# A statically ordered attention and channel-mix kernel: first steps in a new order, measured durations for its scheduler, and two more pairs loaded in blocks

## Chip, cores, metric

The kernel runs on one core of a Trainium2 chip. The metric is the device time of one execution in microseconds (us). Engines are written as in the profile: PE is TensorE (matmul), PEld its weight load, DVE VectorE, ACT ScalarE, POOL GpSimd, SPq the queue of SyncE, which issues most transfers. A position such as "at 40 us" is a time from the start of the profiled execution.

## The reference

Attention over 4 batches and 8 heads, 768 positions, head size 64, in which a query sees only keys of its own cluster; then an RWKV channel mix.

```python
q_assign = argmax(normalised q . normalised centroids)      # 16 clusters per head
k_assign = argmax(normalised k . normalised centroids)
scores = where(q_assign == k_assign, q @ k.T / 8, -1e9)
x = (softmax(scores) @ v), heads put side by side           # 4 x 768 x 512
xk = mu_k * x + (1 - mu_k) * x_prev                         # x_prev: one position earlier
xr = mu_r * x + (1 - mu_r) * x_prev
out = sigmoid(xr @ w_r) * (relu(xk @ w_k) ** 2 @ w_v)
```

## The kernel before

The 32 heads are worked off as 16 pairs (pair 0 to 15, four to a batch). Each pair runs a chain over five engines. The cluster equality is made part of the score matmul: the one-hot cluster rows of q and k are laid under the 64 rows of q and k, so that the contraction has 80 rows. To get the one-hot rows there, they make a "hop": SyncE writes them to DRAM (`hop<-oht`) and reads them back in another layout (`aug<-hop`).

```python
# rows layout (pairs 0 to 5): 2 loads of 384 KB, TensorE transposes, copies from PSUM
eng.dma_start(t[:, i, :]..., src[b, 2*j:2*j+2].rearrange("h (m p r) d -> p (h m) (r d)", p=128, r=2))
nc.tensor.matmul(ps[...], nat[n][:, g // 2, m:m + 128], ident, is_transpose=True, ...)   # trans_pe
# block layout (pairs 6 to 15): 8 loads of 96 KB in 128-byte pieces, VectorE transposes 32x32 blocks
nc.sync.dma_start(nat[n][32*a:32*a+32, i, :]..., x[a // 2, a % 2])                        # load_qk
nc.vector.transpose(qkT[n][:, g, :], nat[n][:, g // 2, ...])                              # trans
# then, for every pair
nc.gpsimd.tensor_scalar(augs[n % NR][0:64, g, par, :], in0=qkT[n][...], ...)              # casts, 8 of them
nc.tensor.matmul(ps[32*g:32*g+32, :], cblk[...], qkT[n][:, g, :], ...)                    # aff_mm
...  # aff_t, aff_max, aff_back on VectorE
nc.sync.dma_start(hop, aff[n])                                                            # hop_out
nc.sync.dma_start(augs[n % NR][64:64 + C]..., hop...)                                     # hop_in
nc.gpsimd.tensor_copy(vts[n % NR][...], vnat[n][...])                                     # vcast
...  # scores (PE), exps (ACT), values (PE), norm (DVE), xtr/xcopy, diff, lerp: xk and xr
```

The order in which each engine takes these pieces of work is made by a small list scheduler in the kernel's Python, when the kernel is built. Every piece of work has an engine, an assumed duration, dependencies and priorities; the scheduler simulates the engines and emits each piece at the earliest time it finds. On the chip each engine then runs its list strictly in that order and waits on semaphores where data is late.

```python
def plan(rings, held, free, moving, at):
    bus = dict(at=at)
    ...
        if k.key in moving:                       # a transfer
            bus["at"] = max(bus["at"], free[e] + 0.4) + moving[k.key]
            k.end = bus["at"] + 1.5
        else:
            k.end = free[e] + k.lat
...
task(("exp", t), "ACT", 0.525, lambda t=t: exps(t), deps=[("scores", t)], ...)
task(("vcast", n), "POOL", 1.2, lambda n=n: vcast(n), deps=[("vload", n)] + ..., ...)
```

The softmax here doesn't subtract the row's maximum and nothing guards it: scores larger than these inputs give would overflow.

Of the kernel before, what the change touches and what calls it, by code (L numbers as in the profile page):

```python
# [16 lines left out]
def kernel(  # L17
# [13 lines left out]
    nc = tc.nc  # L31
# [182 lines left out]
    def first_trans(t):  # L214
        if t == 0:
            qkT[0] = qktp.tile([128, 4, GW], F32, name="qkT")
        for i in range(2):
            g = 2 * i + t
            ps = ps_w.tile([128, GW], F32, name="trps0", tag="w") if t == 0 else \
                (ps_o.tile([128, GW], F32, name="trps1", tag="out2") if i == 0 else  # L220
                 ps_st.tile([128, GW], F32, name="trps2", tag="st"))
            for c2 in range(NCH // 2):
                m = t * GW + c2 * 128
                nc.tensor.matmul(ps[:, c2 * 128:(c2 + 1) * 128], nat[0][:, i, m:m + 128], ident,
                                 is_transpose=True, start=(c2 == 0), stop=(c2 == NCH // 2 - 1))
            if i == 0:
                nc.vector.tensor_copy(qkT[0][:, g, :], ps)
            else:
                nc.scalar.copy(qkT[0][:, g, :], ps)
            casts(0, g)  # L230

    def first_aff(t, i):
        if i == 0:
            first[t] = ps_w.tile([128, 2, NCH, C], F32, name="aff0", tag="w")
        ps = first[t]
        for c2 in range(NCH // 2):
            nc.tensor.matmul(ps[:, i, 2 * c2:2 * c2 + 2, :], qkT[0][:, 2 * i + t, c2 * 128:(c2 + 1) * 128],
                             cblk[:, t, :, :], start=True, stop=True)
# [221 lines left out]
    WK, WR, WV = 11.5, 36.0, 42.0  # L460
    TAIL = {"PE": 0.25 + MARGIN, "ACT": 0.2 + MARGIN, "DVE": 0.15 + MARGIN, "POOL": 0.15, "SP": 0.0}

    def plan(rings, held, free, moving, at):

# [12 lines left out]
        bus = dict(at=at)  # L477
# [36 lines left out]
        while done < len(order):  # L514
# [19 lines left out]
            if k.key in moving:  # L534
                bus["at"] = max(bus["at"], free[e] + 0.4) + moving[k.key]
                k.end = bus["at"] + 1.5
# [20 lines left out]
    with tc.manual_schedule():  # L557
# [11 lines left out]
        load_rows(2, nc.sync, nc.sync)  # L569
        make_identity(nc, ident)  # L570
        init_ring(0)
        nc.gpsimd.tensor_copy(identb, ident)
        def use_pe(m):
# [4 lines left out]
        use_pe(8)  # L578
# [15 lines left out]
        nc.tensor.transpose(cnt_ps.rearrange("d h c -> d (h c)"), cn_sb, ident)  # L594
        nc.vector.tensor_copy(cblk[0:64, :, 0, :], cnt_ps)
        nc.vector.tensor_copy(cblk[64:128, :, 1, :], cnt_ps)
        first_trans(0)
        use_pe(4)
        first_aff(0, 0)
        first_aff(0, 1)  # L600
        first_max(0)
        first_trans(1)
        use_pe(1)
# [3 lines left out]
        for i in range(1, NR):  # L607
            init_ring(i)
        for mu in (mu_k_sb, mu_r_sb):
            nc.vector.tensor_scalar(mu, in0=mu, scalar1=-1.0, scalar2=None, op0=ALU.add)  # L610
# [21 lines left out]
        def soon(n, near, far):  # L632
            return lambda at: near if n < NP or START[n] + 14 <= at else far

        T0 = 10.5
        task(("aff1", 0), "PE", 1.45, lambda: (first_aff(1, 0), first_aff(1, 1)), rank=0, new=[("w", "aff1")],
             uses=[("qkT", 0)], sub=-8)
        task(("aff1max",), "DVE", 0.7, lambda: first_max(1), deps=[("aff1", 0)], uses=["aff1"], rank=0, sub=-8)
        for i in range(2):
            task(("oh1", i), "PE", 0.4, lambda i=i: first_onehot(1, i), deps=[("aff1max",)], rank=0, sub=-8,  # L640
# [3 lines left out]
        task(("vcast", 0), "POOL", 1.2, lambda: vcast(0), rank=0, sub=10, uses=[("vnat", 0)])  # L644

        for n in range(1, NPAIR):
            rows = n < 6
# [3 lines left out]
            if n > 2:  # L651
# [4 lines left out]
                else:  # L656
                    for a in range(8):
                        task(("load", n, a), "SP", 0.6, lambda n=n, a=a: load_qk(n, a // 4, a % 4), rank=2, step=START[n] + 3 * a // 2,
                             sub=due[n], new=[("nat", ("nat", n))] if a == 0 else [], uses=[("nat", n)] if a else [],
                             behind=[("load", n, a - 1)] if a else [("load", n - 1) if n == 6 else ("load", n - 1, 7)])  # L660
                        moving["load", n, a] = 0.65
            task(("vload", n), "SP", 0.5, lambda n=n: load_v(n, nc.sync), rank=2, sub=due[n] + 4, step=due[n] - 16,
                 new=[("vnat", ("vnat", n))], behind=[("vload", n - 1)] if n > 1 else [])
            moving["vload", n] = 1.3
            task(("vcast", n), "POOL", 1.2, lambda n=n: vcast(n), deps=[("vload", n)] +
                 [("norm", k[1] // NCH) for k in old], uses=[("vnat", n)], rank=1, sub=due[n] + 2)
            qt = ("qkT", n)
            if rows:
                at = {1: 10.0, 2: 14.0}.get(n, 0.0)
                for t3 in range(3):  # L670
# [5 lines left out]
                    task(("tcp", n, t3), ce, 0.66 if ce == "DVE" else 0.52,  # L676
# [4 lines left out]
            else:  # L681
                for g in range(4):
                    task(("trn", n, g), "DVE", 0.55, lambda n=n, g=g: trans(n, g),
# [4 lines left out]
            for g in range(4):  # L688
                task(("cast", n, g), "POOL", 1.12, lambda n=n, g=g: casts(n, g), deps=[got[g]] + old, uses=[qt],
# [3 lines left out]
            task(("afft", n), "DVE", 0.6, lambda n=n: aff_t(n), deps=[("aff", n)], uses=[("affps", n)],  # L693
                 new=[("t1", ("t1", n))], rank=0, sub=sub)
            task(("affm", n), "DVE", 1.15, lambda n=n: aff_max(n), deps=[("afft", n)], uses=[("t1", n)],
                 new=[("ohn", ("ohn", n))], rank=soon(n, near, 3 if far else 0), sub=sub)
            task(("affb", n), "DVE", 0.58, lambda n=n: aff_back(n), deps=[("affm", n)], uses=[("ohn", n)],
# [13 lines left out]
        for t in range(NSTEP):  # L711
# [3 lines left out]
            task(("scores", t), "PE", 0.225, lambda t=t: scores(t), deps=need, behind=[("scores", t - 1)] if t else [],  # L715
                 new=[("st", ("st", t))], rank=0, sub=t)
            task(("exp", t), "ACT", 0.525, lambda t=t: exps(t), deps=[("scores", t)], uses=[("st", t)],
# [23 lines left out]
        for b in range(B):  # L741
            for hf in range(NTH):
                X, R, K2 = ("xk", b, hf), ("xr", b, hf), ("k2", b, hf)
                for j in range(NP):
                    n = b * NP + j
                    old = [("lerpr", n - NR, NTH - 1)] if n >= NR else []
                    if b < BX:
                        task(("xtr", n, hf), "PE", 0.14, lambda n=n, hf=hf: xtr(n, hf), deps=[("norm", last[n, hf])],
                             uses=[("xn", n, hf)], new=[("w", ("xps", n, hf))], rank=1, sub=0)
                        task(("xcp", n, hf), "DVE", 0.3, lambda n=n, hf=hf: xcopy(n, hf), deps=[("xtr", n, hf)] + old,  # L750
# [5 lines left out]
                    if hf:  # L756
                        task(("edge", n, hf), "POOL", 0.1, lambda n=n, hf=hf: edge(n, hf), deps=[("xcp", n, hf - 1)] + old,
# [95 lines left out]
```

## Time and profile before

| kernel before | us |
|---|---|
| time, median of 3 runs | 260.63 |
| profiled execution, span | 256.2 |
| first score matmul, first exponential | 12.60, 13.02 |
| first exponential of pair 1 (the 19th) | 28.02 |
| first matmul of the channel mix | 55.1 |
| last matmul starts | 251.7 |

The prediction shows the busy shares, the stretches and the timeline (start, length, engine, line, operation, tiles, count). Two more views matter later. The first is the page's chain that ended last, by engine, and the row of the group of affinity matmuls (line, engine, operation, tiles, shapes, count, busy time and mean ns of one, idle time before them and what ended it):

```profile
PE 70%; DVE 10%; POOL 8%; DMA 6%; issue 2%; ACT 1%; SPq 1%; DVEq 0%; ACTq 0%; POOLq 0%
...
L179 PE MATMUL affps<-qkT,cblk 128*32 128x384 f32 x120 | 14.7, 498 | 0.9 <-DVE qkT L139 0.8
```

TensorE is 70% of the path to the end and transfers are 6%. The second is the timeline of GpSimd (start, length, engine, line, operation, tiles, count):

```profile
12.74 1.81 POOL L613 DMA_DIRECT2D w_k_sb<-in_moe_w_k_dram  x3
14.60 0.95 POOL L170 CAST vt<-v_nat 128x384 bf16<-128x384 f32 x2
15.49 0.53 POOL L613 DMA_DIRECT2D w_k_sb<-in_moe_w_k_dram  x1
16.09 9.51 POOL L163 TENSOR_SCALAR aug<-qkT 64x384 bf16<-64x384 f32 x16
```

After the first weight loads GpSimd casts v of pair 0 and then goes through 16 casts of pairs 1 and 2.

### The profile page before, as it was taken

To read this page: it belongs to the slowest core of one execution; us is meant where nothing else is said; L and a number is where in the kernel's file an instruction comes from. 1 tells how busy PE (TensorE), PEld (TensorE's weight loads), DVE (VectorE), ACT (ScalarE), POOL (GpSimd) and SP (SyncE) were. 2 spreads that over 40 slices of the span, in tenths; PEclk is the share of its full clock that TensorE was granted. 3 is DMA by queue.
4 is the path that set the end of the run, shared out by engine and by line. 5 is a ranking of instruction groups with operands and counts; after the bars stand their busy time and mean duration, and the time that the engine had idled before them with its cause. 6 is when DMAs were issued, how large, how long until landed. Compare 5 with 4: busy or idle time off the path is not lost.

```text
span 256.2 us, 7178 instructions
## 1 busy us (share of the span) xinstructions
PE 243.1 (95%) x2678; PEld 176.1 (69%) x2678; DVE 185.1 (72%) x457; ACT 192.8 (75%) x370; POOL 101.9 (40%) x221
## 2 busy tenths in 40 slices
PE   8999769999999999999998997999999999999993
PEld 4876548987678568767873865687787695666561
DVE  3458687999896989879967996799756566532331
ACT  4298677997899889889995998499899892443440
POOL 1698938681751755455166256335200000000000
PEclk9999998999999999999999999799999999999999
DMA  6997399996579867578997477863511221121112
GB/s 158 280 259 170 110 259 182 206 176 107 120 157 155 140 129 183 107 174 163 146 162 148 94 161 117 182 122 96 152 58 22 61 65 51 43 82 74 49 43 82
DMA packets 106290, 33.60 MB, mean 131 GB/s; under 512 B 75792, under 2 KB 102672, under 8 KB 106256
## 3 DMA queue, kind: packets, MB, share of 16 engines
q1 hardware_dynamic: 102192, 30.13, 54.3%
q0 software_dynamic: 2208, 2.62, 5.9%
q10 hardware_dynamic: 1856, 0.40, 0.8%
q8 instruction: 21, 0.34, 0.6%
q14 instruction: 13, 0.11, 0.2%
HBM read 25.63 MB, written 7.77 MB: 130 GB/s over the span
## 4 chain that ended last, share of the span: by engine, by line
PE 70%; DVE 10%; POOL 8%; DMA 6%; issue 2%; ACT 1%; SPq 1%; DVEq 0%; ACTq 0%; POOLq 0%
PE st L292 18%; PE mw L394 11%; PE mw L423 11%; PE out L311 10%; POOL aug L163 6%; PE mw L410 3%; PE mst L423 3%; PE affps L179 3%; PE mst L394 3%; DMA aug<-hop 2%; DMA qk_nat<-in_q_dram 2%; PE mst L410 2%; PE wps L576 2%; DVE xk L385 2%; DVE qkT L139 2%
## 5 line engine op out<-in xcount | busy, mean ns | idle before, releaser
L299 ACT ACTIVATE pt<-st 128x512 bf16<-128x512 f32 x288 | 152.1, 626 | 24.5 <-PE st L292 23.8
L292 PE MATMUL st<-aug 80*128 80x256 bf16 x576 | 93.7, 275 | 2.1 <-DMA aug<-hop 0.9
L163 POOL TENSOR_SCALAR aug<-qkT 64x384 bf16<-64x384 f32 x128 | 70.5, 550 | 40.6 <-DVE qkT L139 17.2
L292 PEld LDWEIGHTS <-aug 80*128 80x128 bf16 x576 | 50.3, 98 | 26.8 <-issue 12.8
L311 PE MATMUL out<-vt,pt 128*128 128x65 bf16 x1152 | 51.6, 194 | 1.9 <-DVE xn L327 1.9
L311 PEld LDWEIGHTS <-pt 128*128 128x128 bf16 x1152 | 48.2, 97 | 5.1 <-DVE xn L327 2.0
L394 PE MATMUL mw<-xk,w_k_sb 128*128 128x256 bf16 x320 | 40.5, 272 | 0.0
L394 PEld LDWEIGHTS <-w_k_sb 128*128 128x128 bf16 x384 | 36.9, 97 | 5.2
L423 PE MATMUL mw<-w_v_sb,k 128*128 128x512 bf16 x152 | 38.9, 385 | 0.0
L404 DVE TENSOR_TENSOR k<-kr 128x512 bf16<-128x512 bf16 x48 | 22.3, 465 | 11.0 <-ACT kr L400 10.9
L423 PEld LDWEIGHTS <-k 128*128 128x128 bf16 x192 | 18.3, 98 | 17.0 <-issue 0.6
L170 POOL CAST vt<-v_nat 128x384 bf16<-128x384 f32 x32 | 16.8, 552 | 33.0 <-DMA v_nat<-in_v_dram 32.7
L400 ACT ACTIVATE kr<-mw 128x512 bf16<-128x512 f32 x40 | 24.9, 624 | 4.9 <-PE mw L394 4.6
L385 DVE SCALAR_TENSOR_TENSOR xr<-diff,mu_r_sb,xt 128x256 bf16<-128x256 bf16 x48 | 25.0, 526 | 0.0
L139 DVE STREAM_TRANSPOSE qkT<-qk_nat 128x384 f32<-128x384 f32 x40 | 22.5, 565 | 3.3 <-DMA qk_nat<-in_k_dram 1.5
L379 DVE TENSOR_TENSOR diff<-xt 128x256 bf16<-128x256 bf16 x48 | 16.0, 336 | 12.2 <-DMA xt<-xn 9.3
L385 DVE SCALAR_TENSOR_TENSOR xk<-diff,mu_k_sb,xt 128x256 bf16<-128x256 bf16 x48 | 23.7, 499 | 0.3
L429 DVE SCALAR_TENSOR_TENSOR out_sb<-tanh,mw 128x512 f32<-128x512 bf16 x19 | 12.9, 679 | 12.1 <-PE mw L423 10.1
L327 DVE TENSOR_TENSOR xn<-out,rs 128x256 bf16<-128x256 f32 x46 | 19.5, 424 | 1.6
L360 POOL COPY xt<-xt 128x1 bf16<-128x1 bf16 x32 | 6.8, 218 | 33.2 <-DMA xt<-xn 32.1
L179 PE MATMUL affps<-qkT,cblk 128*32 128x384 f32 x120 | 14.7, 498 | 0.9 <-DVE qkT L139 0.8
L410 PE MATMUL mw<-w_r_sb,xr 128*128 128x512 bf16 x56 | 14.4, 378 | 0.0
(66 smaller groups left out, 183.2 us busy)
## 6 DMA issues: line engine op xcount, KB each, us to landing
v_nat<-in_v_dram SPq DMA_DIRECT2D x16, 384.0 KB, 4.8
out_dram<-out_sb SPq DMA_DIRECT2D x24, 256.0 KB, 2.2
qk_nat<-in_q_dram SPq DMA_DIRECT2D x40, 96.0 KB, 3.1
qk_nat<-in_k_dram SPq DMA_DIRECT2D x40, 96.0 KB, 3.7
qk_rows<-in_q_dram SPq DMA_DIRECT2D x5, 384.0 KB, 6.5
qk_rows<-in_k_dram SPq DMA_DIRECT2D x5, 384.0 KB, 6.6
hop<-oht SPq DMA_DIRECT2D x15, 96.0 KB, 2.2
aug<-hop SPq DMA_DIRECT2D x15, 96.0 KB, 2.9
```

The lines of the kernel that those rows point to most:

```text
L139: nc.vector.transpose(qkT[n][:, g, :], nat[n][:, g // 2, (g % 2) * GW:(g % 2 + 1) * GW])
L163: nc.gpsimd.tensor_scalar(augs[n % NR][0:64, g, par, :], in0=qkT[n][64 * par:64 * par + 64, g, :], scalar1=qk_scale, scalar2=1.0, op0=ALU. ...
L179: nc.tensor.matmul(ps[32 * g:32 * g + 32, :], cblk[:, 2 * j + g % 2, :, :], qkT[n][:, g, :], start=True, stop=True, tile_position=(0, 32 * g))
L292: nc.tensor.matmul(st[:, s, :].rearrange("p (r u) -> p r u", r=2), a[rows, 2 + tt, c // (NCH // 2), (c % (NCH // 2)) * 128:(c % (NCH // 2) ...
L299: nc.scalar.activation(pt, sts.pop(t), AF.Exp, bias=-BIG, scale=BIG)
L311: nc.tensor.matmul(o[:, i, :], pts[g * NCH + c][:, s, qc * 128:(qc + 1) * 128], vts[n % NR][:, tt, 2 * (c % 3) + c // 3, 0:D + 1], start=( ...
L385: nc.vector.scalar_tensor_tensor(out=dst[:, j, :], in0=self.d, scalar=mu[:, j:j + 1], in1=xcur(n, self.hf), op0=ALU.mult, op1=ALU.add)
L394: nc.tensor.matmul(ps[:, i * QT:(i + 1) * QT], w_k_sb[:, j, (2 * i2 + i) * 128:(2 * i2 + i + 1) * 128], self.xk[:, j, :], start=(j == 0), ...
L400: nc.scalar.activation(self.kr[i2], self.ps.pop(i2), AF.Relu, scale=0.5 ** 0.5)
L404: nc.vector.tensor_tensor(self.k2[:, 2 * i2:2 * i2 + 2, :].rearrange("p i u -> p (i u)"), kr, kr, op=ALU.mult)
L410: nc.tensor.matmul(ps, self.xr[:, j, sl], w_r_sb[:, j, :], start=(j == 0), stop=(j == NJ - 1))
L423: nc.tensor.matmul(self.ps["v", c], self.k2[:, i, sl], w_v_sb[:, i, :], start=(i == 0), stop=(i == NI - 1))
```

## The change

Four parts, all in the order of work; the arithmetic stays.

1. First steps: k of head 0 is transposed ahead of the centroids, 6 warm-up matmuls (matmuls on zeros, whose results nobody reads) in place of 13 (8, then 4, then 1), the scheduled part starts at 8.7 in place of 10.5 us.
2. The scheduler is given measured durations, and a new model of transfers: two queues (SyncE's and GpSimd's) that overlap at 1.4 times the time, in place of one bus.
3. Pairs 4 and 5 are loaded in blocks.
4. The load of v of pair 1 moves into the fixed first part.

```diff
-        use_pe(8)
+        use_pe(6)
+        first_trans(0, 1)
 ...
-        use_pe(4)
+        first_aff(0, 1)
         first_aff(0, 0)
-        first_aff(0, 1)
         first_max(0)
-        first_trans(1)
-        use_pe(1)
 ...  (other first steps cut)
+        load_v(1, nc.sync)
 ...
-    WK, WR, WV = 11.5, 36.0, 42.0
+    WK, WR, WV = 13.0, 34.0, 40.0
 ...
-                bus["at"] = max(bus["at"], free[e] + 0.4) + moving[k.key]
-                k.end = bus["at"] + 1.5
+                begin = max(queue[e], free[e] + 0.4)
+                both = queue["POOL" if e == "SP" else "SP"] > begin
+                queue[e] = begin + moving[k.key] * (1.4 if both else 1.0)
+                k.end = queue[e] + 1.4
 ...
-            rows = n < 6
+            rows = n < NP                                   # NP is 4
 ...
-            task(("vcast", n), "POOL", 1.2, lambda n=n: vcast(n), deps=[("vload", n)] +
+            task(("vcast", n), "POOL", 1.05, lambda n=n: vcast(n), deps=([("vload", n)] if n > 1 else []) +
 ...
-            task(("exp", t), "ACT", 0.525, lambda t=t: exps(t), deps=[("scores", t)], uses=[("st", t)],
+            task(("exp", t), "ACT", 0.48, lambda t=t: exps(t), deps=[("scores", t)], uses=[("st", t)],
 ...  (some 15 more durations cut)
-        held = {..., "vnat": [("vnat", 0)], ...}
+        held = {..., "vnat": [("vnat", 0), ("vnat", 1)], ...}
```

## The prediction

> **What bounds the kernel now.** I read the page's shares first, then its slices, then a table of stretches that I cut where the slices change, then the timeline inside the stretches that looked bad. The page says that TensorE is busy for most of the span, and where not:
>
> ```profile
> PE 243.1 (95%) x2678; PEld 176.1 (69%) x2678; DVE 185.1 (72%) x457; ACT 192.8 (75%) x370; POOL 101.9 (40%) x221
> ...
> PE   8999769999999999999998997999999999999993
> ...
> PEclk9999998999999999999999999799999999999999
> ```
>
> The dips are at slices 4 to 6 (26 to 38 us) and at 25 (160 us); the clock dips follow the PE dips. The table of stretches (columns: stretch, its length, busy time of each engine, granted clock, DMA share, GB/s) puts sizes on them:
>
> ```profile
> 0.00:12.60 12.60, 11.41 (x71) 7.96 (x72) 5.42 (x19) 4.51 (x6) 5.35 (x24) 1.00 0.86 218
> 12.60:24.40 11.80, 11.69 (x146) 9.09 (x147) 8.35 (x17) 11.29 (x22) 10.74 (x27) 1.00 1.04 236
> 24.40:28.00 3.60, 2.04 (x38) 1.27 (x31) 3.50 (x9) 0.00 (x0) 3.27 (x7) 1.00 0.21 63
> 28.00:33.70 5.70, 5.06 (x56) 3.31 (x54) 2.93 (x12) 5.67 (x12) 4.99 (x11) 1.00 0.63 178
> 33.70:36.10 2.40, 0.29 (x3) 0.04 (x2) 2.27 (x7) 1.78 (x4) 0.00 (x0) 1.00 1.18 243
> 36.10:41.40 5.30, 5.30 (x52) 4.89 (x53) 4.02 (x9) 2.77 (x5) 3.90 (x8) 0.68 1.15 223
> 41.40:55.10 13.70, 13.70 (x217) 11.32 (x215) 12.74 (x34) 13.53 (x27) 10.37 (x22) 1.00 1.13 188
> ...
> 155.00:165.00 10.00, 8.24 (x87) 5.10 (x86) 6.57 (x19) 6.24 (x12) 6.14 (x13) 0.83 0.66 125
> ```
>
> The reader is to see three regimes. (1) Up to 12.6 us there is no score matmul at all; PE looks busy with warm-up matmuls. (2) From 12.6 to 55.1 us ScalarE's exponentials should set the pace (27 in 13.7 us), yet ScalarE stands for the whole of 24.4 to 28.0 and half of 33.7 to 41.4. (3) From 55.1 us on, where the first matmul of the channel mix stands in the timeline, PE is full. Adding up start-to-start times of the matmuls there gives 196.5 us of work between 55.1 and 252 us; all above the back-to-back pace is about 7 us, and over half of it lies at 158 to 164 us. So the end is set by when the channel mix can start, plus some 196 us of PE work, plus holes, plus 4.1 us after the last group (the chain's last piece ends a PE group at 252.1 of 256.2).
>
> The timeline gives the cause of the standstill at 24.4 to 28.0 us:
>
> ```profile
> 20.99 0.34 SPq L205 DMA_DIRECT2D hop<-oht  x1
> ...
> 25.01 0.34 SPq L209 DMA_DIRECT2D aug<-hop  x1
> ...
> 27.61 1.03 PE L292 MATMUL st<-aug 80*128 80x256 bf16 x8 [0.76 <-DMA aug<-hop]
> ...
> 28.02 7.46 ACT L299 ACTIVATE pt<-st 128x512 bf16<-128x512 f32 x15 [3.67 <-PE st L292]
> ```
>
> Pair 1's cluster rows leave at 20.99 us, take 4.0 us to DRAM and 2.5 back; ScalarE has by then run out of pair 0. The landings show why the first leg took 4.0 us where later ones at a quiet queue took 1.6: the loads of v for pairs 1 and 2, issued on the same queue at 12.3 and 13.6 us, landed at 23.4 and 24.8, beside 1 MB of w_k that landed between 18.4 and 24.1.
>
> **What the Trainium skill says.** "TensorE: Matmul & The Clock Gate", section "HAM oscillation — how this bites in real kernels": long idle gaps bring TensorE down to half clock. The trace agrees: its two half-clock stretches inside the run, 3.41 us each (37.5 to 40.9 and 160.4 to 163.8), follow the holes at 33.7 and 158.0; each costs about 1.7 us where PE is full. The same page, "Part 4: PE-mode transpose": the result goes to PSUM and needs a VectorE copy. Here 60 transposes of 292 ns mean and 15 copies (12 on VectorE, 680 ns) do it. "DMA: Bandwidth & Descriptors", "Issuing engines are not separate DMA queues": loads from SyncE and GpSimd share the 16 engines. The trace agrees: the DMA share is over 1.0 in 12.6 to 24.4 and 33.7 to 55.1 us, and landings there take 5 to 11 us against 2 to 3 elsewhere. Same page, "Why small descriptors are slow (HBM only)": a fixed cost per packet. The trace's packet records on the SyncE queue: 128-byte packets 14.3 ns, 512-byte 31.3 ns, so 1.8 times the time per byte.
>
> **The change, part by part.**
>
> *First steps.* Seven of 13 warm-up matmuls go (8+4+1 to 6). The last five stand on the path: 4 between the transposes and the first affinities (6.07 to 7.46), one before the one-hots. k is transposed before the centroids, since its load landed at 3.71 us while TensorE played warm-ups until 4.5. The channel-mix constants' two DVE operations (0.63 us) leave this place. Affinities of head 1 no longer go ahead of the first scores. The schedule's own start goes from 10.5 to 8.7 us, the first score from 12.6 (trace) to 9.4 allowed. I count -2.5 us for the first exponential (13.0 to about 10.5). Against it: with fewer warm-ups PE may get its full clock later (it came at 6.8 us); the 12 affinities of 112 ns and 12 one-hot transposes of 56 ns would then double, an estimated 1 to 2 us. The author's 8.7 suggests that it doesn't happen fully.
>
> *Pair 1.* GpSimd is back to back from 10.05 to 32.4 us. It now has its ring fills (12.35 to 12.8) out of the way and starts head 1's casts about 1.7 us sooner; v of pair 1 is issued before the crowd and v of pair 2 after it, so the hop should find fewer bytes before it. The rows should start 2 us sooner and land 1 to 2 us faster: pair 1's first score at about 23.5 in place of 27.6 us, **-4 us**, which includes the 2.5 above. The w_k loads still stand beside it, so I don't count the full standstill away.
>
> *The hole at 33.7.* PE waits 2.1 us for a norm that VectorE has queued behind a difference, which waits 2.7 us for a one-column copy that GpSimd has queued behind v casts. It is an order that followed from wrong durations (plan: exponential 0.525 us; trace: 0.477 back to back). With measured ones I expect most of it, and the half clock that follows, to go: **-1.5 us**; ScalarE bounds this stretch, so not the full 2.3 + 1.7.
>
> *Pairs 4, 5 in blocks.* PE: 2 pairs x 12 transposes x 0.109 us start to start = 2.6 us less. VectorE: 6 copies x 0.680 = 4.1 us go, 8 transposes x 0.565 = 4.5 us come. But both pairs' transposes lay at 36 to 48 us, mostly where ScalarE paces: in 41.4 to 55.1 its 28 exponentials lose 0.7 us in all to late scores. So **-0.7 us**. DMA: 2 x (6144 x 14.3 - 1536 x 31.3)/16 = +5 us of every engine, put where the share is already 1.1: up to **+0.5 us** through later w_v or hops, which have slack.
>
> *Order of the rest.* 196 us of PE work stay. The hole at 158 us (1.9 us, plus 1.7 of half clock) came from a VectorE transpose waiting 1.5 us for block loads with norms queued behind it. A new order moves this; equally late transfers can open another. I count **-1.5 us** of 3.6.
>
> Sum: -4 -1.5 -0.7 +0.5 -1.5 = -7.2 us; on 260.6 this is 253.4. I shade it to 253.
>
> **Rivals.** *GpSimd or the hop still sets pair 1's start*: casts 8 x 0.57 us per pair, v casts and w_k issues are all still there, and data of pair 1 lands at 10.5 us whatever the order. For it: the chain of waits in 9 to 60 us has 28.6% in these casts. Against: it starts sooner. Then the gain at the start is 1.5 us only: about 257. *New holes in the dense part*: shorter durations make a tighter static order, and each engine obeys it even when a transfer is late. For it: the larger PE holes after 80 us go back to a DMA landing of 3 to 6 us, and the plan now allows 1.4 after the queue. One hole costs 1 to 2 us, with a half-clock stretch 3 to 4: 256 to 258. *All holes go*: first exponential at 10.4 + 64 exponentials x 0.477 + 3 us of copies by ScalarE + 3 of waits puts the channel mix at 47 to 48 us instead of 55.1, then 196 + 4 + little: 248 to 249.
>
> **Range and chances.** 2% is 255.4 us. The most certain part (start, 2.5) doesn't reach it alone; two of the others have to come with it, and they are all of a kind that measured durations should mend. 253.0 us, 248.5 to 258 holds it 8 times in 10. Faster by over 2%: 0.73; within 2%: 0.24; slower: 0.03.
>
> **What would show it.** First score by 10.5 and first exponential by 11; pair 1's first score by 24 and ScalarE idle before it under 2 us; no PE hole over 1 us at 30 to 40; first channel-mix matmul at 48 to 51 us; x36 row transposes and x48 stream transposes; at most one half-clock stretch after 30 us. Wrong: the channel mix starts early but the end doesn't move as far (new holes), or half clock lasting to 10 us.

## The result and the profile after

The changed kernel takes 269.08 us (median of 4, 267.49 to 270.17) against 260.05 (258.35 to 261.64) for the kernel before in the same rounds. The ratio is 1.034 (1.026 to 1.043): slower, where I had predicted a gain of about 3%. Here and below a ratio is the mean time of one kernel's fast runs over that of the other's fast runs of the same rounds, so it is not quite the ratio of the medians; the brackets are 95% intervals. Executions over 1.5% slower than the fastest of the same kernel are left out of the means.

The two profiles side by side, with a second profile of the changed kernel (e5 below). All three are fast runs.

| us from the start | before | after | after, second profile |
|---|---|---|---|
| first score, first exponential | 12.60, 13.02 | 10.05, 10.47 | 10.38, 10.79 |
| first exponential of pair 1 (19th) | 28.02 | 29.45 | 29.37 |
| 31st exponential | 33.8 | 35.5 | 35.3 |
| 43rd | 43.4 | 45.9 | 43.0 |
| rows of pair 4 back from the hop | 58.8 | 67.5 | 66.2 |
| 73rd (pair 4's first) | 62.7 | 69.2 | 66.8 |
| first channel-mix matmul | 55.1 | 62.2 | 56.9 |
| first channel-mix result | 65.0 | 77.5 | 75.7 |
| last exponential | 210.1 | 215.6 | 214.7 |
| last matmul | 251.7 | 264.0 | 263.1 |
| span | 256.2 | 268.2 | 267.3 |

The gain of the first steps is there (2.5 us at the first exponential) and is gone at pair 1. By the first result of the channel mix the kernel is 12.5 us behind (10.7 in the second profile), and it ends 12.0 (11.1) behind. This suggests that all of the loss is made in the first 78 us, but the first result is a weak mark, since it depends on the order too: in e7 below it comes 7.6 us later than in before, and the kernel ends 1.6 us later. An estimate from the matmuls, which both profiles hold in full (2678 in before; after has the 7 warm-ups and 24 transposes fewer, 2647): priced at the start-to-start times of before, the changed kernel has some 8 us more of TensorE's work left at 78 us, and some 4 us more go lost after that.

The page of the kernel after shows the same rows as the prediction's first fence, then the chain and the affinity group that were shown of before:

```profile
PE   7994973998999989999898999999999999999994
...
PEclk9998998589999999999999999999999999999998
...
PE 50%; DMA 20%; DVE 10%; SPq 8%; POOL 6%; issue 3%; ACT 1%; DVEq 0%; ACTq 0%; POOLq 0%
...
L179 PE MATMUL affps<-qkT,cblk 128*32 128x384 f32 x120 | 20.1, 525 | 2.2 <-DVE qkT L139 2.2
```

TensorE has new dips at slices 4 and 7 (20 to 27 and 40 to 47 us) and a clock of 5 tenths at slice 8. In the chain TensorE has fallen from 70 to 50%, and transfers with SyncE's issuing have grown from 7 to 28%. The same 120 affinity matmuls of nearly the same length cover 20.1 us in place of 14.7.

A table of stretches of the kernel after (columns as in the prediction: stretch, length, busy time of PE, PEld, DVE, ACT and POOL, granted clock, DMA share, GB/s):

```profile
20.90:24.70 3.80, 0.05 (x1) 0.00 (x0) 0.71 (x2) 0.71 (x2) 3.30 (x8) 0.96 0.90 190
24.70:29.00 4.30, 3.76 (x38) 2.72 (x38) 3.82 (x8) 2.44 (x5) 3.79 (x8) 0.64 0.78 154
...
41.00:45.00 4.00, 0.00 (x0) 0.00 (x0) 3.31 (x9) 0.52 (x2) 3.44 (x7) 0.99 1.26 176
45.00:55.10 10.10, 9.95 (x86) 6.87 (x87) 5.08 (x16) 5.60 (x11) 5.24 (x10) 0.50 1.30 156
```

Two standstills of TensorE of about 4 us, each followed by half clock. The second half-clock stretch lasts 10.2 us, and the 10.1 us of the last line get only 86 matmuls done; the kernel before got 217 done in the 13.7 us from 41.4.

**The first standstill, at 20.9.** The timeline of GpSimd after, to be read against the four lines shown of before:

```profile
11.78 0.95 POOL L170 CAST vt<-v_nat 128x384 bf16<-128x384 f32 x2 [1.22 <-DMA v_nat<-in_v_dram]
15.68 0.96 POOL L170 CAST vt<-v_nat 128x384 bf16<-128x384 f32 x2 [2.95 <-DMA v_nat<-in_v_dram]
16.72 1.27 POOL L163 TENSOR_SCALAR aug<-qkT 64x384 bf16<-64x384 f32 x2
18.03 1.81 POOL L622 DMA_DIRECT2D w_k_sb<-in_moe_w_k_dram  x3
```

GpSimd stands 1.22 and 2.95 us for v (the brackets: idle time before, and what ended it), with the casts of pair 1 and the w_k loads queued behind. The scheduler took v of pair 1 for present and had its cast end at 12.05 us (GpSimd's start at 8.7 + 1.1, two casts of 1.05, 0.15 of latency); it ends at 16.6. w_k is issued at 18.03 in place of 12.74 and now moves together with v of pair 2 (issued 18.56, landed 28.39) just ahead of the rows of pair 1, whose second leg takes 9.0 us (19.92 to 28.90; before 25.01 to 27.47). The first leg had left earlier than in before, at 18.18 in place of 20.99.

The table of waits of the kernel after from 15 to 62 us (who waited for what: us in total, times, longest):

```profile
ACT pt L300 <- PE st L293: 10.9, 7, 4.3
...
DVE qkT L159 <- POOL aug L163: 5.3, 1, 5.3
PE st L293 <- DMA aug<-hop: 5.1, 2, 4.6
```

The second line is the first standstill: a copy on VectorE waits for GpSimd's casts, and TensorE waits for VectorE. In the same stretch of before, ScalarE's wait in the first line was 6.9 us and the third was 0.8.

**The second standstill, at 40.6.** That is the third line: TensorE waits 4.6 us for the rows of pair 3. The timeline of SyncE's queue shows what stands in front of them:

```profile
34.28 0.52 SPq L205 DMA_DIRECT2D hop<-oht  x1
34.85 1.41 SPq L84 DMA_DIRECT2D qk_nat<-in_q_dram  x2
36.30 3.54 SPq L84 DMA_DIRECT2D qk_nat<-in_k_dram  x4
39.94 0.47 SPq L209 DMA_DIRECT2D aug<-hop  x1
```

The first leg left at 34.28 and landed at 38.82. The second was ready to go then, but SyncE was still issuing six block loads of pair 4 and came to it at 39.94; it landed at 45.11, behind those loads. The Trainium skill, "DMA: Bandwidth & Descriptors", section "Queues, rings and completion order", says that each of the 16 engines consumes a queue's descriptors in ring order. This trace agrees: the six block loads, issued from 34.85 to 39.31, landed at 39.36 to 43.50, and the hop issued after them at 45.11. In the kernel before, pair 3's second leg was issued at 31.35, before any block load:

```profile
29.31 0.32 SPq L205 DMA_DIRECT2D hop<-oht  x1
...
31.35 0.91 SPq L209 DMA_DIRECT2D aug<-hop  x1
```

These two lines also show that most of the delay is older than the block loads. The rows of pair 3 are 7.3 us late (45.11 against 37.81), and 5.0 us of that are there when the first leg leaves (34.28 against 29.31). In e4 and e10 below, where pair 4 comes in rows again, pair 3's rows are back at 43.7 and 43.0, hardly sooner; in e1, where one cast on GpSimd is moved, at 40.1. So the lateness of pair 3 is for the larger part a result of the first standstill. Whether TensorE then stands depends on the plan: in e4 and e10 it has no wait over 1 us for these rows.

**The rows of pair 4.** They leave at 56.06 and land at 62.5, go again at 63.64 and land at 67.5; before 48.92 to 55.0, then 55.71 to 58.8. Both profiles of the changed kernel have this delay, while the 10 us of half clock are in the first alone (3.4 us in the second). Pair 4's first exponential is late with it (by 6.5 and 4.1 us). What that costs is not shown: TensorE has other work until then and no wait for these rows in the first profile (1.3 us in the second), and in the profile of e8 below the rows are just as late (67.7), while the first channel-mix result (65.5) and the last matmul (251.8) stand where they stand in before.

**Affinities in the dense part.** The view of the tile of affinities (idle time of its engine before it, times, and what ended it), before and after:

```profile
  DVE qkT L139: 3.1, 3
```

```profile
  DVE qkT L139: 9.7, 13
```

The four groups of a pair's affinity matmuls come one behind each of VectorE's four transposes. Start to start, the affinities after the channel mix had begun cost 10.5 us in before and 16.5 us after, for 80 matmuls each. The Trainium skill, "Perfetto Trace Analysis", section "Identifying the Most-Contended Engine", warns that matmul busy time says little about how near one is to the bound. Here busy time even rises, because matmuls that overlapped no longer do. Against it stand the hole at 158 us and its half clock, 3.6 us together, which are gone.

### The profile page after: what moved, and what is told of

It reads as the page before. It is cut to its first block, busy times and chain, and to the rows that moved or that the text cites.

```text
span 268.2 us, 7146 instructions
## 1 busy us (share of the span) xinstructions
PE 246.3 (92%) x2647; PEld 174.3 (65%) x2647; DVE 183.9 (69%) x459; ACT 192.8 (72%) x370; POOL 102.8 (38%) x221
## 3 DMA queue, kind: packets, MB, share of 16 engines
q1 hardware_dynamic: 111600, 30.13, 56.2%
## 4 chain that ended last, share of the span: by engine, by line
PE 50%; DMA 20%; DVE 10%; SPq 8%; POOL 6%; issue 3%; ACT 1%; DVEq 0%; ACTq 0%; POOLq 0%
PE st L293 12%; PE mw L424 7%; DMA qk_nat<-in_k_dram 7%; PE out L312 7%; PE mw L395 6%; DMA xt<-xn 6%; SPq L84 5%; PE mst L395 5%; POOL aug L163 5%; PE mw L411 4%; PE mo L424 3%; DMA aug<-hop 3%; PE affps L179 3%; DMA v_nat<-in_v_dram 2%; DVE qkT L139 2%
## 5 line engine op out<-in xcount | busy, mean ns | idle before, releaser
L300 ACT ACTIVATE pt<-st 128x512 bf16<-128x512 f32 x288 | 153.1, 638 | 30.1 <-PE st L293 26.0
L312 PE MATMUL out<-vt,pt 128*128 128x65 bf16 x1152 | 54.6, 196 | 1.0 <-DVE xn L328 1.0
L312 PEld LDWEIGHTS <-pt 128*128 128x128 bf16 x1152 | 50.9, 99 | 5.3 <-issue 1.3
L424 PE MATMUL mw<-w_v_sb,k 128*128 128x512 bf16 x144 | 36.0, 379 | 0.0
L139 DVE STREAM_TRANSPOSE qkT<-qk_nat 128x384 f32<-128x384 f32 x48 | 27.3, 570 | 11.8 <-DMA qk_nat<-in_k_dram 11.6
L395 PE MATMUL mw<-xk,w_k_sb 128*128 128x256 bf16 x264 | 34.0, 272 | 0.6 <-ACT kr L401 0.6
L170 POOL CAST vt<-v_nat 128x384 bf16<-128x384 f32 x32 | 16.5, 544 | 40.0 <-DMA v_nat<-in_v_dram 39.9
L401 ACT ACTIVATE kr<-mw 128x512 bf16<-128x512 f32 x33 | 21.1, 638 | 13.3 <-PE mw L395 13.0
L380 DVE TENSOR_TENSOR diff<-xt 128x256 bf16<-128x256 bf16 x48 | 15.2, 317 | 12.3 <-DMA xt<-xn 10.6
L179 PE MATMUL affps<-qkT,cblk 128*32 128x384 f32 x120 | 20.1, 525 | 2.2 <-DVE qkT L139 2.2
L411 PE MATMUL mw<-w_r_sb,xr 128*128 128x512 bf16 x76 | 19.5, 379 | 0.0
```

What stands on the lines that cost most here:

```text
L139: nc.vector.transpose(qkT[n][:, g, :], nat[n][:, g // 2, (g % 2) * GW:(g % 2 + 1) * GW])
L179: nc.tensor.matmul(ps[32 * g:32 * g + 32, :], cblk[:, 2 * j + g % 2, :, :], qkT[n][:, g, :], start=True, stop=True, tile_position=(0, 32 * g))
L300: nc.scalar.activation(pt, sts.pop(t), AF.Exp, bias=-BIG, scale=BIG)
L312: nc.tensor.matmul(o[:, i, :], pts[g * NCH + c][:, s, qc * 128:(qc + 1) * 128], vts[n % NR][:, tt, 2 * (c % 3) + c // 3, 0:D + 1], start=( ...
L395: nc.tensor.matmul(ps[:, i * QT:(i + 1) * QT], w_k_sb[:, j, (2 * i2 + i) * 128:(2 * i2 + i + 1) * 128], self.xk[:, j, :], start=(j == 0), ...
L401: nc.scalar.activation(self.kr[i2], self.ps.pop(i2), AF.Relu, scale=0.5 ** 0.5)
```

## The experiments

Eighteen kernels ran; all results were correct. They were run in five calls on three chips (12, 10, 5), with the kernel before in each. Before's fast runs had means of 256.3, 256.2, 257.7, 258.4 and 258.1 us and 260.0 in the first result; the changed kernel had 269.0 and 269.5. So absolute means are compared where two kernels ran on one chip, and ratios otherwise. In some of them the profiled run is left out, which moves them by 0.2 points at most, but for e1. Below, "mean" is that of the fast runs. Letters in the expectations stand for theories; the line that heads each experiment says in words what is tested (D is the late full clock, E the two-queue transfer model).

### One move in the finished order

The scheduler was run with the changed kernel's input, its order kept, and one piece of work moved before emitting. This separates a bad place in the order from a new plan.

**e1_v1cast**: is the cast of v in front of pair 1's casts what costs the gain at the start?

```diff
+        put(("vcast", 1), ("cast", 1, 3))        # in the emitted sequence: behind pair 1's casts
```

> The changed kernel with one move in its fixed order: the cast of v of pair 1 stands behind pair 1's q/k casts on GpSimd, nothing else is reordered. Theory A (GpSimd's head of line: it stood 2.95 us for this v load, and w_k, pair 1's casts and all behind it came late): GpSimd's wait goes, w_k is issued at about 13 to 15 us in place of 18, pair 1's first score comes at 23 to 25 us in place of 29.0, and the kernel gains 3 to 5 us on the changed one (264 to 266). Theory B (the loss is made at 40 to 55 us by block loads around the hop of pair 3): pair 1 starts sooner but the hole at 40 us takes most of it back, gain under 2 us. Theory C (the loss is spread over a tighter order): no change over 1 us.

Measured: 265.80, 267.65 fast, two slow at 270.2; mean 266.7, which is 1.041 of before's 256.3. The ratio, 1.052 (1.043 to 1.060), leaves out the profiled 265.80 and counts the two at 270.2 as fast. So a gain of 2.8 us on the changed kernel (269.5 in e5, same chip) or none: unclear. In its profile the w_k loads go at 13.5, pair 1's first exponential comes at 26.87 (after: 29.45), the channel mix starts at 55.7. So the place of this cast did delay pair 1 by 2.6 us. The end moves by less: TensorE still waits 2.4 us for pair 3's rows (second leg issued at 35.0, landed at 40.1), and pair 4's come at 63.3.

**e2_hop3**: are the block loads in front of pair 3's second leg the cause?

```diff
+        for a in range(7, 0, -1):
+            put(("load", 4, a), ("hop2", 3))     # pair 4's block loads behind pair 3's second leg
```

> The changed kernel with one move: seven of the eight block loads of pair 4 stand behind the second leg of pair 3's hop on the SyncE queue. Theory B: the PE hole of 4.75 us at 40.4 us shrinks to under 1.5 us, and the half clock from 44.9 to 55.1 us goes or shrinks to one stretch of 3.4 us; gain 5 to 8 us (261 to 264). Theory A: the hole at 20.7 us stays, pair 1 still at 29.0, and as pair 3 is late from there, gain 1 to 3 us. A side effect to watch: pair 4's data comes some 4 us later.

Measured: 269.62, 269.50 fast, 275.62 and 288.84 slow; ratio 1.052 (1.044 to 1.061). Nothing gained. Its profile fell in a slow run (clock 0.85), so it says only this much: the wait at 40 us is gone and another of 3.3 us, for a norm, stands at 45.0.

**e3_both**: both moves.

> Both moves together. If A and B are two separate causes the gains add: 256 to 260 us. If the second is only a result of the first (pair 3 late because GpSimd was late), this is no faster than the better one of the two alone.

Measured: 266.04, 265.25 fast, 276.23 and 275.70 slow; mean 265.6; ratio 1.037 (1.028 to 1.046). Two thirds of the loss are left with both places mended. The profile, of a slow run, again shows a new hole (5.8 us at 44.4). This suggests that mending one place lets the next late thing stand there; as both profiles are of slow runs, in which the full clock came only at 23.3 and 23.5 us, it is not shown.

**e4_rows45**: the changed kernel planned anew, with pairs 4 and 5 in rows as before.

```diff
-            rows = n < NP
+            rows = n < 6
-  [("load", n - 1) if n == NP else ("load", n - 1, 7)]
+  [("load", n - 1) if n == 6 else ("load", n - 1, 7)]
```

> The changed kernel with pairs 4 and 5 loaded in rows and transposed on TensorE as before, everything else of the change kept, order planned anew. If the block loads are what costs (theory B): 260 to 263 us, no long half clock at 45 to 55. If the start costs (theory A): 266 to 269, pair 1's first score still at 29 us. TensorE has 2.6 us more work, which both theories hold to be hidden there.

Measured: 264.36, 262.85 fast, 268.05 and 268.34 slow; mean 263.6; ratio 1.029 (1.020 to 1.038). Some 6 us of the loss go with the blocks (against e5's 269.5 on the same chip). Pair 4's rows are back at 59.9. In this profile, of a fast run, TensorE got its full clock only at 17.3 us and the first score came at 13.74 (e2 and e3: 13.8 and 13.9); that brought the question of the warm-ups.

### Warm-ups, and the changed kernel again

**e5_after_again**: the changed kernel unaltered, 5 rounds: is its time one group or two, and is its start cold?

> The changed kernel once more, unaltered, to see how its start falls: three of the four kernels of the first batch kept half clock until 17 to 24 us (warm-up matmuls 427 ns apart and no full-clock record before), the changed kernel's own profile got full clock at 3.9 us. Theory D (with 6 warm-ups it is chance whether TensorE's clock comes up at 4 or at 17 to 24 us): the times fall into two groups some 4 to 8 us apart, 266 to 269 and 272 to 277. If D is wrong: one group.

Measured: 268.44 to 270.87 in five fast runs, 272.94 slow; ratio 1.053 (1.047 to 1.059). One group. The profile has the full clock at 5.9 us and the first score at 10.38.

**e6_warm**: the changed kernel with before's warm-ups.

```diff
-        use_pe(6)
+        use_pe(8)
+        use_pe(4)                                # before the first affinities
+        use_pe(1)                                # before the one-hots
```

> The changed kernel with the 13 warm-up matmuls of before (8, 4 and 1) in the new order of first steps, nothing else. Theory D: full clock by about 7 us in every run, one group of times, first score at 10.5 to 11.5 us; no run over 270; median as good as the better group of the unaltered one or 1 us above it. If warm-ups don't matter: all times about 1 to 1.5 us longer.

Measured: 267.98 to 270.62 in five fast runs, mean 268.8; ratio 1.050 (1.044 to 1.055). One execution, the profiled one, took 485.48 us, with no record of a full clock in it. That one is set aside; it is also the only profile of e6. In the others the warm-ups are worth nothing here: 0.7 us against e5, inside the intervals. A likely reason, not shown, is that the start is hidden behind v and the hop.

### A kernel with all suspected places mended, and its parts

**e7_warm_rows_v**: the changed kernel with 13 warm-ups, pairs 4 and 5 in rows, and the scheduler told when v lands. I call it the mended kernel.

```diff
 (e4's and e6's edits, and:)
-  ("vcast", 0) ... uses=[("vnat", 0)])
+  ("vcast", 0) ... uses=[("vnat", 0)], after=11.5)
-  ("vcast", n) ... sub=due[n] + 2)
+  ("vcast", n) ... sub=due[n] + 2, after=15.4 if n == 1 else 0.0)
```

> The changed kernel with three parts undone: 13 warm-ups, pairs 4 and 5 in rows, and the planner told that v of pairs 0 and 1 lands at 11.5 and 15.4 us (it takes them for present); order planned anew. Theories A, B and D together explain the loss: 253 to 258 us, at or under the kernel before. Theory C (the measured durations make an order that is too tight): still 262 or more.

Measured: 257.19 to 260.34 in four fast runs, two slow to 261.84; mean 258.8; ratio 1.011 (1.004 to 1.017). Over 10 us of the loss are gone (e5: 269.5, same chip). TensorE is at full clock from 5.1 us to the end. It is still not faster than before. Pair 1 comes at 27.36, only 0.7 us earlier than in before, because the first leg of its hop takes 5.0 us (19.3 to 24.3) beside w_k; attention is then 6.6 us ahead at the 73rd exponential (56.1), and yet the channel mix starts at 56.2. From 35 to 55 us VectorE is busy for 19.56 of 20 us (before 17.66), and the last xk that the mix needs comes at 54.3.

**e8_before_blocks**: the kernel before with block loads for pairs 4 and 5 alone.

```diff
-            rows = n < 6
+            rows = n < NP
```

> The kernel before with only pairs 4 and 5 in block loads, order planned anew. Theory B: 3 to 7 us slower than before, pair 4's rows land later than 58.8 us by 3 us or more, channel mix starves at 55 to 65 us. If blocks cost nothing by themselves: within 1 us.

Measured: 257.90, 261.64, 260.75 fast, 264.66 slow; mean 260.1; ratio 1.016 (1.007 to 1.024). By the means the blocks cost 3.9 us on the kernel before too, though the three runs lie 3.7 us apart. Pair 4's rows come at 67.7, as late as in the changed kernel; but the profiled run is the fastest, 257.90, and has no loss to show, so it doesn't tell where the 3.9 us go.

**e9_warm_v**: the mended kernel with the blocks put back.

```diff
-            rows = n < 6
+            rows = n < NP
```

> The repaired kernel (13 warm-ups, rows for pairs 4 and 5, planner told of the v landings; 1.011 of before) with the block loads of pairs 4 and 5 put back. Theory B (block loads crowd the hops of pairs 3 and 4): 3 to 7 us slower than the repaired one, ratio 1.025 to 1.04. Theory A (the v cast is the cause, block loads harmless once GpSimd is on time): ratio 1.01 to 1.015.

Measured: 271.52, 273.50, 269.66 fast, three slow to 275.75; mean 271.6; ratio 1.054 (1.047 to 1.062). That is 4.3 points over e7 on another chip, some 11 us, and as slow as the changed kernel. The waits of TensorE from 20 to 100 us, first of e7, then of e9 (the profiled e9 was a slow run by its time, 274.76, at a clock of 0.975, so the size is rough):

```profile
PE st L293 <- DMA aug<-hop: 2.3, 2, 2.0
```

```profile
PE st L293 <- DMA aug<-hop: 12.2, 4, 4.0
```

With blocks the scores wait four times for rows on the hop. Pair 4's first leg takes 7.1 us (52.82 to 59.95), and when it has landed SyncE is still issuing block loads, one of which takes 3.37 us to issue; the second leg goes at 63.47.

**e10_warm_rows**: the mended kernel without being told when v lands.

> The repaired kernel with only the v landings untold again, so that GpSimd stands for v of pair 1 ahead of pair 1's casts. Theory A: 3 to 5 us slower than the repaired one, ratio 1.022 to 1.03, w_k issued at 18 us instead of 15, pair 1's first exponential 1.5 to 3 us later. Theory B: within 1 us of the repaired one.

Measured: 262.77 to 265.64 in five fast runs, one slow; mean 264.0; ratio 1.025 (1.019 to 1.031). 1.4 points over e7, on another chip. w_k goes at 18.1 again and pair 1 comes at 29.46, as in the changed kernel.

**e11_rows_v**: the mended kernel with 6 warm-ups.

> The repaired kernel with 6 warm-ups in place of 13. Theory D (late full clock is a matter of chance with 6): two groups of times, one as good as the repaired kernel or 1 us better, one 4 to 8 us slower. If warm-ups don't matter on the clock: one group, about 1 us faster than the repaired kernel.

Measured: 259.37 to 262.64 in four fast runs, 264.08 and 269.53 slow; mean 261.4; ratio 1.015 (1.008 to 1.021). 0.4 points over e7: within the intervals, so nothing is shown for the warm-ups.

**e12_warm_rows_v_old**: the mended kernel with the old durations and the one-bus model, so parts 1 and 4 of the change alone (with before's 13 warm-ups, and the scheduler told when v lands).

> The repaired kernel planned with the old durations and the old model of one DMA bus, so that of the change only the order of the first steps and the early load of v of pair 1 are left. Theory C (the measured durations make a worse order, in which VectorE's work for later pairs goes ahead of the channel mix's operands): faster than the repaired one by 2 us or more, ratio 0.99 to 1.0, first channel-mix matmul by 53 us instead of 56. If the measured durations help: ratio 1.015 or more.

Measured: 262.28 to 264.64 in four fast runs, two slow; mean 263.3; ratio 1.020 (1.015 to 1.026). With the new first steps the old durations are a point worse than the measured ones (e7, on another chip), with intervals that overlap. So measured durations are not shown to be bad in themselves. Nor is this a clean test of them: in the profile of e12 pair 1's first leg lands at 23.53, but its second is issued only at 27.03, behind pair 2's first leg (26.59), and pair 1 starts at 30.1 in place of 27.4.

### What of the block loads costs time

**e13_pieces128**: the mended kernel; pairs 4 and 5 keep rows and TensorE transposes, but are loaded by 8 transfers of 96 KB in 128-byte pieces, as blocks are.

```diff
+    def load_piece(n, i, a):                     # 32 columns of every row
+        s = slice(32 * a, 32 * a + 32)
+        nc.sync.dma_start(t[:, :, s], x[:, :, s])
```

> The repaired kernel, pairs 4 and 5 still in row layout and transposed on TensorE, but each loaded by 8 DMAs of 96 KB in pieces of 128 bytes, as many and as small as the block loads. If the transfers are what costs (packets or issues): ratio 1.03 to 1.055, legs of the hops of pairs 3 and 4 take 7 to 8 us as with the block loads. If VectorE's transposes or their place in its order cost: ratio 1.005 to 1.02, as the repaired kernel.

Measured: 268.27 to 269.24 in six fast runs, mean 268.7; ratio 1.040 (1.032 to 1.047). VectorE's transposes of pairs 4 and 5 aren't needed for the loss. In the timeline of VectorE:

```profile
58.66 0.58 DVE L148 STREAM_TRANSPOSE qkT<-qk_nat 128x384 f32<-128x384 f32 x1 [6.83 <-DMA qk_nat<-in_k_dram]
```

VectorE stands 6.83 us for a block load of pair 6 that is late, with an xk of the channel mix two places behind it in its list. TensorE waits 6.64 us for that xk. The expected sign did not come, however: the legs of pairs 3 and 4 took 3.3 to 5.2 us, not 7 to 8. So the transfers alone cost 2.9 points over e7 (another chip), but here by another path than the hops.

**e14_pieces512**: the same 8 transfers, cut so that the pieces are 512 bytes.

```diff
-        nc.sync.dma_start(t[:, :, s], x[:, :, s])
+        nc.sync.dma_start(t[s], x[s])            # 32 partitions, whole rows
```

> As e13, with 8 DMAs of 96 KB by groups of 32 partitions, so pieces of 512 bytes. If the size of the packets costs: ratio 1.005 to 1.02. If the number of issues on the SyncE queue costs: 1.03 to 1.055, like e13.

Measured: 262.88 to 266.65 in five fast runs, one slow; mean 265.0; ratio 1.028 (1.016 to 1.040). 3.7 us less than with small pieces, and 1.7 points more than e7 on another chip. The intervals overlap, so the split between the number of transfers and the size of their pieces stays open; both may count.

### The durations and the transfer model

**e15_b_durations**: the kernel before with part 2 alone.

> The kernel before with the measured durations, the two-queue DMA model and the new times for the weights alone. If these are a gain by themselves (the repaired kernel lost 1 per cent when they were taken out): ratio 0.98 to 0.995, a version that beats both. If they only help together with the new first steps: 1.0 to 1.01.

Measured: 265.20 to 268.63 in six fast runs, mean 266.8; ratio 1.033 (1.023 to 1.042). Before's own order of first steps, v loads and rows, and 8.4 us slower. The timeline of VectorE in it:

```profile
56.55 0.58 DVE L139 STREAM_TRANSPOSE qkT<-qk_nat 128x384 f32<-128x384 f32 x1 [3.37 <-DMA qk_nat<-in_k_dram]
```

The same picture as in e13: the plan let this transpose go ahead of an xk, because it thought the load present; TensorE then waits 3.86 us for the xk.

**e16_vlate**: the mended kernel with v of pair 1 loaded by the scheduler, as before.

> The repaired kernel with v of pair 1 loaded as before, by the plan, not in the first steps. If the early v load crowds what pair 1 needs: faster than the repaired kernel, 0.99 to 1.005. If it helps or does nothing: 1.01 to 1.02.

Measured: 259.10 to 262.31 in five fast runs, one slow; mean 260.6; ratio 1.009 (0.998 to 1.019). The same as e7: once the scheduler knows when v lands, moving the load is worth nothing that can be seen.

**e17_b_dur_bus**: e15 with the one-bus model, so the durations and weight times alone.

```diff
-                begin = max(queue[e], free[e] + 0.4)
-                both = queue["POOL" if e == "SP" else "SP"] > begin
-                queue[e] = begin + moving[k.key] * (1.4 if both else 1.0)
-                k.end = queue[e] + 1.4
+                bus["at"] = max(bus["at"], free[e] + 0.4) + moving[k.key]
+                k.end = bus["at"] + 1.5
```

> The kernel before with the measured durations, but with its own model of one DMA bus. Theory E (the two-queue model promises data too soon): ratio 1.0 to 1.015, no wait of VectorE over 2 us for a block load before the first channel-mix matmul. If the durations themselves make the order worse: 1.025 to 1.04, as e15 (1.033).

Measured: 260.54 to 263.68 in five fast runs, one slow; mean 262.2; ratio 1.016 (1.010 to 1.023). On the kernel before, about half of part 2's loss goes with the transfer model and half with the durations (on two chips).

**e18_after_bus**: the changed kernel with the one-bus model. If the two-queue model (theory E) is at fault, this must be faster than the changed kernel.

> The changed kernel with the one-bus DMA model of before, block loads, durations and first steps kept. Theory E: 1.01 to 1.03 in place of 1.034 to 1.053, and the waits of TensorE for the hops of pairs 3 and 4 under 3 us together. If the block loads cost whatever the plan knows: 1.04 to 1.055, hops as late as before.

Measured: 270.92 to 273.82 in six fast runs, mean 272.5; ratio 1.057 (1.051 to 1.062). It is not faster. That does not settle theory E, because the new plan brought a new fault: pair 1's first leg lands at 21.90, its second is issued at 28.38, behind pair 2's first leg (27.94), and pair 1 starts at 33.1 in place of 29.4. The waits of TensorE over 1 us for the rows of pairs 3 and 4 are gone, as theory E expected. What the transfer model alone is worth in the changed kernel stays open.

### What the runs add up to

| what | measured as | cost in points of ratio |
|---|---|---|
| blocks for pairs 4, 5 on the mended kernel | e9 against e7 | 4.3 |
| the same on the kernel before | e8 | 1.6 |
| the same, taken from the changed kernel | e5 against e4 | 2.4 |
| v's landing not told | e10 against e7 | 1.4 |
| durations and model, on before | e15 | 3.3 |
| the same, with the new first steps | e7 against e12 (intervals overlap) | -1.0 |
| 6 warm-ups for 13 | e11 against e7; e5 against e6 | 0.4; 0.3 |

They are not additive: each row was planned anew, and a new plan moves the waits. How far a new plan by itself moves the time was not measured. No order that was tried was faster than the kernel before; e16, the nearest, can't be told from it.

## Why the prediction was wrong

It gave 253.0 us (248.5 to 258), with 0.03 for slower. Going through its own sum:

**First steps: -2.5, right.** The first exponential came at 10.47, predicted "about 10.5"; the clock question didn't spoil it in the two profiles of the changed kernel. With the same six warm-ups it did in three others (e2, e3, e4): full clock at 17.3 to 23.5 us and the first exponential at 14.4 to 14.5, later than in before. In the changed kernel the gain is gone by pair 1.

**Pair 1: -4, got +1.4.** The first half of this step came true: GpSimd starts head 1's casts at 8.35 in place of 10.05 us, the 1.7 us of the prediction, and pair 1's rows leave 2.8 us sooner. The failing step is that they would then "land 1 to 2 us faster" because "the hop should find fewer bytes before it": from leaving to landing they took 10.7 us in place of 6.5. I read from the diff that v of pair 1 is issued earlier, but not that its cast lost its dependency, so that the plan would put it in front of pair 1's casts while the data lands at 15.6 us. GpSimd's wait of 2.95 us, the w_k loads 5.3 us later, and the hop's second leg of 9.0 us follow. e1 gives 2.6 us back at pair 1's first exponential by moving that one cast, and e10 against e7 shows it as 1.4 points of the time. The rival "GpSimd or the hop still sets pair 1's start" was right, and undersized: it kept a gain of 1.5 us.

**Hole at 33.7: -1.5.** That hole did not recur, as predicted, and the stretch was not better for it: TensorE stood 4.6 us from 40.6 (2.1 in the second profile) for pair 3's rows, late for the larger part because pair 1 was. The reading of "HAM oscillation" fits in kind only: that section speaks of gaps over about 3.4 us, while the two holes of before that half clock followed are 2.1 and 1.8 us of idle TensorE.

**Pairs 4, 5 in blocks: -0.7 +0.5, the largest error.** The failing step is "later w_v or hops, which have slack". Counted by engines, the swap is as I had it: 36 row transposes and 48 stream transposes stand in the page, and TensorE has less work. But the hops run in the one queue in which blocks of later pairs are issued: pair 4's came back at 67.5 in place of 58.8. Instead of -0.2 us, the blocks cost 5.9 us in the changed kernel (e5 against e4), 3.9 on the kernel before (e8) and 4.3 points, some 11 us, on the mended one (e9 against e7, two chips). That the transfers alone cost most of it on the mended kernel (2.9 of the 4.3 points) is shown by e13; by which wait is not, since e8 has the late rows without a loss in its profile and e13 the loss without slow hops. The load on the transfers was undersized too, though not by enough to explain this: with 54.3% of the span in before and 56.2% after, SyncE's packets took 139.1 and 150.7 us of each DMA engine on average, 11.6 us more where I had worked out 5.

**Order of the rest: -1.5.** The hole at 158 us went, as I had hoped. What I hadn't counted is that affinity matmuls stand behind VectorE's transposes one by one: 6.0 us more, which is more than the hole was worth. "All of a kind that measured durations should mend" is the sentence that failed: part 2 alone makes the kernel before 3.3% slower (e15). A plan made from shorter durations sets each transfer's consumer closer to its assumed landing, and an engine that takes its list in order then holds up everything behind a late one. In e15 and e13 this can be read off: a transpose waits for a load, an xk behind it, TensorE behind that. That it is the general cause is inferred from these two cases.

The rival "new holes in the dense part" was the right one, but I gave it 256 to 258 us; the size wasn't limited to one hole.

**The checks.** First score and first exponential came in time; "pair 1's first score by 24" failed (29.0), and ScalarE stood 6.2 of the 9.4 us before it; "first channel-mix matmul at 48 to 51" failed (62.2 and 56.9), "no PE hole over 1 us at 30 to 40" held, but the next begins at 40.6, "at most one half-clock stretch after 30 us" held in number, and the one lasted 10.2 us. A slip in the working, from which nothing follows: its 28 exponentials between 41.4 and 55.1 us are 27, as in its table.

**What stays open.** Even the mended kernel (e7) doesn't beat before, although its first score comes 1.6 us earlier and its attention runs 6.6 us ahead. VectorE being full from 35 to 55 us is what its profile shows in the way; which change of order would use the lead was not found. Whether before's order is a lucky one among many, so that any new plan loses a per cent or two, is suggested by the fact that none of the orders tried was faster, and not shown.

## What to carry to other kernels

A statically ordered kernel is one object: a new duration or a dependency left out changes every later place, so a gain worked out for one part does not add to the next, and the parts have to be run one at a time. Ask of each added transfer not only how many bytes it moves, but what stands behind it in its queue, and ask of each scheduled consumer whether its dependency on the load is still there. When an engine runs its list in order, the assumed landing time of a transfer should rather be late than early; how late was not tested.

## What the Trainium skill lacked or had wrong

- "DMA: Bandwidth & Descriptors", "Issuing engines are not separate DMA queues", calls the time a sequencer takes to initiate a DMA usually small beside the DMA. Here one issue of a 96 KB block load took SyncE 0.31 to 3.37 us (3.37 at most in the profiles of before and e9, 2.28 in the changed kernel's), and a ready hop behind such issues waited 1.1 us in the changed kernel and 3.5 us in e9.
- The same page has no figure for how long a small transfer waits behind others of its queue. One leg of a hop (96 KB) took from 1.6 us (26.3 to 27.9 in before) to 9.0 us (pair 1's second leg after).
- "TensorE: Matmul & The Clock Gate", "What's actually happening", puts the return to full clock at about 3.4 us of sustained work. It gives no figure for how dense the work must be. With 86 matmuls in 10.10 us, shown as 9.95 us busy, the half clock lasted 10.24 us. And with the same six warm-ups the full clock came between 3.9 and 5.9 us in five profiles (after, e1, e5, e11, e18) and at 17.3 to 23.5 us in three others (e4, a fast run; e2 and e3, slow ones).
- The same page, "Seeing it yourself", mentions a clock gate seen stuck, at a quarter, for 50 us and more. One execution here, of e6, took 485.48 us in place of 269, with no record of full clock and its 512-column matmuls 443 ns apart in place of 216: half clock throughout.
- No page says how an affinity-like group of matmuls shows in the profile when its members wait one by one: busy time rose from 14.7 to 20.1 us for the same 120 matmuls of about 0.5 us.
